# Local attention in 32-query tiles, division at the PV eviction, and norm per token, in a fused attention and two-MLP kernel

## The chip, the cores and the metric

One core of one Trainium2 chip runs the program. The metric is the device time of one execution in microseconds (us); lower is better.

## The reference

```python
# attention, B=4, H=8, Sl=512 local and Sg=32 global tokens, D=64, window 32
s_g = scale * q_g @ k_all.T                      # global queries see all 544 keys
out_g = sm(s_g) @ v_all
s_ll = where(|i - j| <= 32, scale * q_l @ k_l.T, -1e9)
a_l = sm(concat([scale * q_l @ k_g.T, s_ll]))    # local: 32 global keys and a band
out_l = a_l @ concat([v_g, v_l])
x = concat([out_g, out_l]) as (2176 tokens, 512)
# first MLP, F=1536
xn = x / sqrt(mean(x*x) + 1e-6) * rms_g
x = (silu(xn @ w_gate) * (xn @ w_val)) @ w_out
# second MLP, F=2048
out = (s * relu(x @ w_in)**2 + b) @ w_out
# sm(s) = exp(s - max) / (sum + 1e-9)
```

The weights come as 64-bit floats.

## The kernel before

**Dense part.** The 2176 tokens are cut into five groups of 512, 512, 512, 320 and 320 tokens (GROUPS). For each group 12 slots of the first MLP and 16 of the second run one after another; a slot is 128 hidden features. All dense products are split into a high and a low fp32r part and computed as three matmuls (`mm3`, L621 to L624): `emit_first` makes the hidden features into the PSUM tiles `m`, `emit_second` adds them into four banks `acc0` and `acc1`. There are 4128 dense matmuls. During group 0 the weights are loaded as 64-bit values (`load_raw`, into `wr`), converted on ScalarE and VectorE (`conv`, L162 to L198), kept in one of five tiles `wt`, and stored to a scratch `wsc` in DRAM, which the later groups read (`load_w`).

**Attention.** A unit is one batch and two heads. The units of batches 1, 2 and 3 (12 units with local tokens) and the four of batch 0 (global tokens alone) are worked off in small steps between the dense matmuls of the group before the one that needs them (`unit_steps`, `unit_queue`); odd units also do the 32 global queries of two units. The local tokens of batch 0 are done first, in `start`, in eight half units of 256 tokens. The steps of a unit are:

- `sc` (twice): 8 score matmuls of 64 queries by 160 keys (128 of the window, 32 global), both heads and two query blocks side by side in the array; four VectorE operations add the mask and take the minimum (L281).
- `st_e`: eight exponentials with row sums on ScalarE (L331). `st_r`, `st_n`, `glob`: reciprocals, division of the probabilities, on VectorE and ScalarE.
- `st_t` (twice): five transposes (L253, L254), one copy (L257). `st_v`: 16 matmuls of 64 by 64 for the window (L268) and 8 of 64 by 128 for the global keys (L276); the output is feature-major.
- odd units: `st_g`, `st_tg`, `st_gv` (L318, L359, L377) for the global queries.

`build_steps` makes the normed input `x` of a group: squares, one matmul with ones that sums over the partitions (L470; in group 0 four of 256 tokens for each half, L461), a reciprocal root over all tokens on all partitions, one scaling, and the high and low parts. In group 0 it runs once for each 256 tokens, so the first two slots start on the first half (`hs`).

**What sets the order.** The program text gives priorities (`hp`) and dependences; a scheduler that runs before the chip does fixes one order of instructions for each engine. SP issues all DMAs in one such order.

Of the kernel before, what the change touches and what calls it, by code (L numbers as in the profile page):

```python
# [24 lines left out]
KW = 160  # L25
VW = 9 * 128 + 64
# [17 lines left out]
C_ID = 3 * KW  # L44
# [13 lines left out]
SW = 256 + 4 * KW + 4 * 128 + 64  # L58
# [5 lines left out]
def attn_moe_kernel(ctx: ExitStack, tc: tile.TileContext, s0, q, k, v, w1, w2, cst, out):  # L64
# [43 lines left out]
    zeros = cp.tile([128, 128], F32, name="zeros")  # L108
    zw = zeros[:, 0:1].broadcast_to((128, 512))
    epsc = cp.tile([128, 1], F32, name="epsc")  # L110
    pm = cp.tile([128, 4, 2, KW], F32, name="pm")
    pg = cp.tile([128, 640], F32, name="pg")
    qf = cp.tile([128, 2, 64], F32, name="qf")
    ident = ct[:, C_ID:C_ID + 128]
    mask = [ct[:, C_MASK + i * KW:C_MASK + (i + 1) * KW] for i in range(3)]

    def cmask(c):
        return mask[0 if c == 0 else (2 if c == 3 else 1)]
# [88 lines left out]
    def u_tile(b):  # L207
        if b not in ut:
            ut[b] = u_p.tile([128, HP, 4, 128], F32, tag="u", name="u")
        return ut[b]  # L210
# [6 lines left out]
    def load_u(i):  # L217
        if i >= len(UNITS) or i in raw_u:
            return
        b, p, loc = UNITS[i]  # L220
        vr = at_p.tile([128, VW], F32, tag="vr", name="vr", bufs=2)
        e = ST if loc else SG
        qr = at_p.tile([128, ST], F32, tag="qr", name="fq")
        kr = kr_p.tile([128, 8, KW], F32, tag="kr", name="fk")
        nc.sync.dma_start(out=qr[:, 0:e], in_=q[b, p, :, 0:e])
        nc.sync.dma_start(out=kr, in_=k[b, p])
        nc.sync.dma_start(out=vr, in_=v[b, p])
        raw_u[i] = (qr, kr, vr)

    def scores(bk, qr, kr, q0, cs):  # L230
        mms = []
        for n, c in enumerate(cs):
            for e in range(2):
                for h in range(2):
                    x = slice(64 * h, 64 * h + 64)
                    i = 2 * c + e
                    mms.append(PE.matmul(bk[64 * e:64 * e + 64, h, n * KW:(n + 1) * KW],  # L237
                                         lhsT=qr[x, q0 + 64 * i:q0 + 64 * i + 64], rhs=kr[x, i]))
        in_turn(mms)

    def glob(p, rs):
        gl = pt_p.tile([128, 4, 32], F32, tag="gl", name="gl")
        V.tensor_tensor(out=gl, in0=p.rearrange("p c h n -> p (c h) n")[:, :, 128:KW],
                        in1=rs.rearrange("p (n o) -> p n o", o=1).broadcast_to((128, 4, 32)), op=ALU.mult)
        return gl.rearrange("p n k -> p (n k)")

    def transposes(bk, p, gl):
        flat = bk.rearrange("p b n -> p (b n)")
        mms = []
        for c in range(2):  # L250
            for h in range(2):
                o = 128 * (2 * c + h)
                mms.append(PE.transpose(flat[:, o:o + 128], p[:, c, h, 0:128], ident))  # L253
        mms.append(PE.transpose(flat[:, 512:640], gl, ident))  # L254
        in_turn(mms)
        t = pt_p.tile([128, 5, 128], F32, tag="pt", name="ptf")
        A.copy(out=t.rearrange("p a n -> p (a n)"), in_=flat[:, 0:640])  # L257
        return t

    def values(bk, vr, vg, pts):  # L260
        mms = []
        for c in range(2 * len(pts)):
            t = pts[c // 2]
            for e in range(2):
                for h in range(2):
                    i = 2 * c + e
                    o = 128 * (c // 2) + 64 * e
                    mms.append(PE.matmul(bk[64 * h:64 * h + 64, c % 2, o:o + 64],  # L268
                                         lhsT=vr[:, 128 * i + 64 * h:128 * i + 64 * h + 64],
                                         rhs=t[:, 2 * (c % 2) + h, 64 * e:64 * e + 64], start=(c < 2 and e == 0), stop=False))  # L270
        for c in range(2 * len(pts)):
            t = pts[c // 2]
            for h in range(2):
                x = slice(32 * (2 * (c % 2) + h), 32 * (2 * (c % 2) + h) + 32)
                o = 128 * (c // 2)
                mms.append(PE.matmul(bk[64 * h:64 * h + 64, c % 2, o:o + 128], lhsT=vg[x], rhs=t[x, 4],  # L276
                                     start=False, stop=(c // 2 == len(pts) - 1), tile_position=(x.start, 64 * h)))
        in_turn(mms)

    def neg_scaled(out_, in_, m, acc):  # L280
        V.tensor_tensor_reduce(out=out_, in0=in_, in1=m, scale=-0.125, scalar=3.0e38,  # L281
                               op0=ALU.add, op1=ALU.min, accum_out=acc)

    def norm_eng(out_, in_, sc_, e):
        if e == "A":
            A.mul(out=out_, in_=in_, mul=sc_)
        else:
            V.tensor_scalar(out=out_, in0=in_, scalar1=sc_, scalar2=None, op0=ALU.mult)

    def unit_steps(i):  # L290
# [4 lines left out]
        def prep():  # L295
# [5 lines left out]
            S["nm"] = sm_p.tile([128, 4, 2], F32, tag="nm", name="nm")  # L301
# [36 lines left out]
        def st_r():  # L338
# [3 lines left out]
            if not kp:  # L342
                return
# [458 lines left out]
```

## Time and profile before

| | us |
|---|---|
| median of 3 runs (range) | 996.46 (996.26 to 997.35) |
| span of the profiled execution | 995.6 |
| TensorE busy (PE) | 946.3 (95%) |
| weight loads busy (PEld) | 790.7 (79%) |
| VectorE busy (DVE) | 471.7 (47%) |
| ScalarE busy (ACT) | 464.9 (47%) |
| moved by DMA | 249.54 MB |

The page gives the span of the profiled execution, from its first to its last instruction, and no other time for it; the median of the runs lies 0.9 us above. The busy time of PE counts overlapping matmuls once. Matmul records of fp32 operands come in twos: one matmul instruction leaves two records. "at" is a two-bank PSUM tile that all attention steps share, "m" and "acc" hold dense results.

### The profile page before, as it was taken

Reading aid. Unit: us, or ns where it says so; the run is one execution under the profiler, and the core shown is the slowest. Engines: PE = TensorE matmul, PEld = TensorE weight load, DVE = VectorE, ACT = ScalarE, POOL = GpSimd, SP = SyncE. Lnnn points to the kernel's source line nnn. Section 1 sums busy time; section 2 is a strip of 40 time slices with the busy share of each in tenths; the row PEclk is TensorE's granted clock in tenths of the full one; section 3 lists DMA queues with packets and bytes.
Section 4 is the critical chain, followed back from the end, with each engine's and each line's share of the span. In section 5 each row is a group of like instructions: output and inputs, shape, how many; then the busy total and the mean of one; then the engine's idle time right before and its main releaser. Section 6 shows DMA issues by size and latency. Waiting matters only on the chain.

```text
span 995.6 us, 15191 instructions
## 1 busy us (share of the span) xinstructions
PE 946.3 (95%) x6024; PEld 790.7 (79%) x6024; DVE 471.7 (47%) x1149; ACT 464.9 (47%) x908; POOL 0.8 (0%) x9
## 2 busy tenths in 40 slices
PE   5758999889999999999999999999999999999998
PEld 4437777667877778777877878778789999999998
DVE  6995978769954141334353131443442243421322
ACT  5886697667744152533346252633441342311222
POOL 0000000000000000000000000000000000000000
PEclk9578999999999999999999999999999999999999
DMA  9985789848964754446565655346488848988584
GB/s 371 409 324 204 282 306 349 308 162 311 356 240 170 264 203 183 163 143 225 213 232 191 239 204 187 142 173 245 167 308 337 305 159 309 340 338 300 181 328 153
DMA packets 41110, 249.54 MB, mean 251 GB/s; under 512 B 5072, under 2 KB 6096, under 8 KB 23120
## 3 DMA queue, kind: packets, MB, share of 16 engines
q1 hardware_dynamic: 41040, 248.58, 67.4%
q8 instruction: 47, 0.77, 0.3%
q14 instruction: 23, 0.19, 0.0%
HBM read 208.46 MB, written 40.11 MB: 250 GB/s over the span
## 4 chain that ended last, share of the span: by engine, by line
PE 80%; DMA 7%; DVE 6%; ACT 5%; issue 1%; SPq 0%; ACTq 0%; DVEq 0%
PE m L622 15%; PE m L624 14%; PE m L623 14%; PE acc L622 10%; PE acc L623 10%; PE acc L624 10%; DMA wr<-in_w_dram 4%; DMA wt<-wsc 2%; PE at L237 2%; PE at L268 1%; ACT ce L177 1%; PE at L377 1%; PE at L253 1%; DVE wt L142 1%; DMA fq<-in_q_dram 1%
## 5 line engine op out<-in xcount | busy, mean ns | idle before, releaser
L623 PE MATMUL acc<-h,wt 128*128 128x512 f32 (+1 forms) x560 | 200.6, 359 | 1.4 <-DVE h L142 1.3
L624 PE MATMUL acc<-h,wt 128*128 128x512 f32 (+1 forms) x560 | 200.2, 358 | 0.0
L622 PE MATMUL acc<-h,wt 128*128 128x512 f32 (+1 forms) x560 | 192.5, 363 | 0.5 <-DVE y L142 0.3
L622 PE MATMUL m<-x,wt 128*128 128x512 f32 (+2 forms) x496 | 178.7, 362 | 11.3 <-ACT x L136 9.2
L623 PE MATMUL m<-x,wt 128*128 128x512 f32 (+2 forms) x496 | 175.8, 355 | 0.1
L624 PE MATMUL m<-x,wt 128*128 128x512 f32 (+2 forms) x496 | 175.3, 354 | 0.0
L622 PE MATMUL m<-y,wt 128*128 128x512 f32 (+1 forms) x320 | 117.0, 373 | 7.6 <-DVE t L711 4.2
L623 PE MATMUL m<-y,wt 128*128 128x512 f32 (+1 forms) x320 | 116.2, 364 | 2.9 <-DVE y L142 2.9
L623 PEld LDWEIGHTS acc<-h,wt 128*128 128x128 f32 x560 | 105.2, 188 | 15.3 <-DVE h L142 2.1
L622 PEld LDWEIGHTS acc<-h,wt 128*128 128x128 f32 x560 | 103.6, 188 | 16.3 <-issue 1.7
L624 PEld LDWEIGHTS acc<-h,wt 128*128 128x128 f32 x560 | 105.1, 188 | 13.6 <-issue 0.5
L624 PE MATMUL m<-y,wt 128*128 128x512 f32 (+1 forms) x320 | 115.4, 361 | 0.0
L622 PEld LDWEIGHTS m<-x,wt 128*128 128x128 f32 x496 | 93.9, 190 | 26.4 <-ACT x L136 9.9
L692 DVE TENSOR_TENSOR a<-sg,m 128x512 f32<-128x512 f32 (+1 forms) x60 | 36.4, 607 | 142.9 <-PE m L624 136.5
L624 PEld LDWEIGHTS m<-x,wt 128*128 128x128 f32 x496 | 93.9, 189 | 11.1 <-issue 0.3
L623 PEld LDWEIGHTS m<-x,wt 128*128 128x128 f32 x496 | 93.9, 189 | 10.8 <-DVE x L142 0.8
L711 DVE SCALAR_TENSOR_TENSOR t<-m,ct,r 128x512 f32<-128x512 f32 (+1 forms) x80 | 53.2, 670 | 98.3 <-ACT r L710 98.1
L710 ACT ACTIVATE r<-m 128x512 f32<-128x512 f32 (+1 forms) x80 | 42.1, 532 | 115.2 <-PE m L624 115.0
L685 ACT ACTIVATE sg<-m 128x512 f32<-128x512 f32 (+1 forms) x60 | 32.0, 534 | 96.9 <-PE m L624 96.7
L136 ACT CAST h<-a 128x512 fp32r<-128x512 f32 (+1 forms) x60 | 33.3, 555 | 92.2 <-DVE a L692 73.2
L622 PEld LDWEIGHTS m<-y,wt 128*128 128x128 f32 x320 | 59.8, 189 | 20.8 <-ACT y L136 4.4
L713 ACT ACTIVATE h<-t,ct 128x512 fp32r<-128x512 f32 (+1 forms) x80 | 52.2, 658 | 50.9 <-DVE t L711 33.1
(141 smaller groups left out, 1137.6 us busy)
## 6 DMA issues: line engine op xcount, KB each, us to landing
wt<-wsc SPq DMA_DIRECT2D x48, 1536.0 KB, 7.5
wt<-wsc SPq DMA_DIRECT2D x64, 1024.0 KB, 4.8
wr<-in_w_dram SPq DMA_DIRECT2D x68, 512.0 KB, 6.3
wsc<-wt SPq DMA_DIRECT2D x12, 1536.0 KB, 7.3
wsc<-wt SPq DMA_DIRECT2D x16, 1024.0 KB, 6.2
fk<-in_k_dram SPq DMA_DIRECT2D x16, 640.0 KB, 5.3
vr<-in_v_dram SPq DMA_DIRECT2D x16, 608.0 KB, 6.0
s_w<-in_s_dram SPq DMA_DIRECT2D x8, 736.0 KB, 11.5
```

Of the source, the lines that this page charges most:

```text
L136: A.copy(out=out_, in_=in_)
L142: V.tensor_tensor(out=dst_l, in0=src, in1=dst_h.bitcast(F32), op=ALU.subtract)
L177: A.copy(out=e.bitcast(I16), in_=odd)
L237: mms.append(PE.matmul(bk[64 * e:64 * e + 64, h, n * KW:(n + 1) * KW], lhsT=qr[x, q0 + 64 * i:q0 + 64 * i + 64], rhs=kr[x, i]))
L622: PE.matmul(out_, lhsT=wh, rhs=xh, start=first, stop=False)
L623: PE.matmul(out_, lhsT=wh, rhs=xl, start=False, stop=False)
L624: PE.matmul(out_, lhsT=wl, rhs=xh, start=False, stop=last)
L685: A.activation(out=sg[:, :N], in_=gb[:, :N], func=AF.Silu)
L692: V.tensor_tensor(out=a[:, :N], in0=sg[:, :N], in1=vb[:, :N], op=ALU.mult)
L710: A.activation(out=r[:, :N], in_=hb[:, :N], func=AF.Relu)
L711: V.scalar_tensor_tensor(out=t[:, :N], in0=hb[:, :N], scalar=ct[:, C_S:C_S + 1], in1=r[:, :N], op0=ALU.mult, op1=ALU.mult)
L713: A.activation(out=h[:, 0, :N], in_=t[:, :N], func=AF.Identity, bias=ct[:, C_B:C_B + 1])
```

## The change

A local unit is now one block. Queries go in 16 tiles of 32; each sees 64 keys before and 64 after a cut (96 of the window, 32 global: `key_window` takes them as two pieces of one key array, so the block has 128 columns and no separate global part). Scores are 32 matmuls of 32 rows by 128 columns into both banks. The mask is added to the 512 scores per row that need it, one reduction takes the maximum of the eight rows of 128, one subtraction writes all 1024 values, one exponential follows. Eight transposes and one copy turn the unnormed probabilities. PV is 32 matmuls of 32 rows by 65 columns, token-major; the 65th column of V is one and gives the row sum, and the division is done as the result is evicted. The input norm of a group is then a ScalarE square with a row sum per 128 tokens, a reciprocal root of a few columns, a scaling, and 16 transposes per 512 tokens (8 in the groups of 320) before the high and low parts are made. Global tokens get a small norm of their own (`gsq`). In `start` batch 0 is done in four whole units, with loads of its own from `q`, `k` and `v`; `build_steps(0)` runs once, over all 512 tokens. Global PV takes six key blocks in place of five.

```diff
-KW = 160
-VW = 9 * 128 + 64
+KN = 544
+KW = KN + 16 * 64
+VW = 130
+NW = 17
...
-    def scores(bk, qr, kr, q0, cs):
+    def scores(bk, qr, kr, q0):
         mms = []
...
+        for i in range(16):
+            c, g = divmod(i, 4)
+            for h in range(2):
+                x = slice(64 * h, 64 * h + 64)
+                mms.append(PE.matmul(
+                    bk[32 * g:32 * g + 32, h, 128 * c:128 * c + 128].rearrange("p (a n) -> p a n", a=2),
+                    lhsT=qr[x, q0 + 32 * i:q0 + 32 * i + 32], rhs=key_window(kr, x, i)))
         in_turn(mms)
...
+    def less_max(bk, pp):
+        sv = bk.rearrange("p h (c n) -> p (h c) n", n=128)
+        ends = sv.rearrange("p a (b n) -> p a b n", n=64)[:, :, :, 0:32]
+        mx = sm_p.tile([128, 8], F32, tag="mx", name="mx")
+        V.tensor_tensor(out=ends, in0=ends, in1=mask, op=ALU.add)
+        V.tensor_reduce(out=mx, in_=sv, axis=mybir.AxisListType.X, op=ALU.max)
+        V.tensor_tensor(out=pp, in0=sv, in1=mx.rearrange("p (a o) -> p a o", o=1).broadcast_to((128, 8, 128)),
+                        op=ALU.subtract)
...
+    def values(bk, vr, t, o):
         mms = []
...
+        for c in range(4):
             for h in range(2):
+                for g in range(4):
+                    mms.append(PE.matmul(bk[32 * g:32 * g + 32, h, 65 * c:65 * c + 65],
+                                         lhsT=t[:, 4 * h + c, 32 * g:32 * g + 32],
+                                         rhs=vr[:, 4 * c + g, 65 * h:65 * h + 65]))
         in_turn(mms)
...
+        V.tensor_scalar(out=rs, in0=po[:, :, :, 64], scalar1=1e-9, scalar2=None, op0=ALU.add)
+        V.reciprocal(out=rs, in_=rs)
+        V.tensor_tensor(out=o.rearrange("p c (h n) -> p h c n", h=2), in0=po[:, :, :, 0:64],
+                        in1=rs.rearrange("p h (c o) -> p h c o", o=1).broadcast_to((128, 2, 4, 64)), op=ALU.mult)
...
+        r = [(prep, 0.3)]
+        if not loc and not kp:
+            return r + [(lambda: load_u(i + 1), 0.0)]
+        if loc:
+            r += [(st_s, 0.8), (lambda: expo(pm), 2.5)]
+        if kp:
+            r += [(st_g, 0.8), (st_r, 1.5), (st_tg, 1.0), (st_gv, 1.5)]
+        if loc:
+            r += [(st_t, 1.5), (st_v, 1.5)]
+        return r
...
+        def turn(p0, p1):
+            bk = bank().rearrange("p a n -> p (a n)")
+            w = 128 * n
+            in_turn([PE.transpose(bk[:, w * (p - p0) + 128 * (c - c0):w * (p - p0) + 128 * (c - c0) + 128],
+                                  ut[b][:, c, 128 * p:128 * p + 128], ident) for p in range(p0, p1) for c in cs])
+            x = x_tile()
+            for p in range(p0, p1):
+                src = bk[:, w * (p - p0):w * (p - p0) + w]
+                gs = ct[:, C_G + p:C_G + p + 1]
+                A.mul(out=x[:, 0, p, 0:w], in_=src, mul=gs)
+                V.scalar_tensor_tensor(out=x[:, 1, p, 0:w], in0=src, scalar=gs, in1=x[:, 0, p, 0:w].bitcast(F32),
+                                       op0=ALU.mult, op1=ALU.subtract)
...
+            for p in range(HP):
+                PE.matmul(bk, lhsT=ones, rhs=s[:, p], start=(p == 0), stop=(p == HP - 1))
...
+        def ld(u, last=True):
+            qr, kr, vr = raw[u]
+            nc.sync.dma_start(out=qr, in_=q[0, u, :, SG:ST])
+            nc.sync.dma_start(out=kr, in_=k[0, u])
+            if u == 0:
+                nc.sync.dma_start(out=ct, in_=cst)
+            nc.sync.dma_start(out=vr[:, 0:16], in_=v[0, u, :, 0:16])
...
+        with hp(400):
+            for f in build_steps(0, nb):
+                f[0]()
         load_u(0)
```

Two places show how the orders of instructions move. The first is TensorE while group 1 is computed, at the end of an attention unit. Before, the second five transposes and the 24 PV matmuls (L622 to L624 are dense):

```order
L624 MATMUL m<-y,wt 128x512
L253 MATMUL at<-ct,pm 128x128 x4
L254 MATMUL at<-ct,gl 128x128
L622 MATMUL m<-y,wt 128x512 x2
L623 MATMUL m<-y,wt 128x512
L624 MATMUL m<-y,wt 128x512
L623 MATMUL m<-y,wt 128x512
L624 MATMUL m<-y,wt 128x512
L268 MATMUL at<-ptf,vr 64x64 x16
L276 MATMUL at<-ptf,vr 64x128 x8
L622 MATMUL m<-y,wt 128x512
```

Now (L548 to L550 are dense):

```order
L259 MATMUL at<-ct,pm 128x128 x8
L548 MATMUL m<-x,wt 128x512
...
L550 MATMUL m<-x,wt 128x512
L269 MATMUL at<-vr,ptf 32x65 x32
L548 MATMUL acc_2843<-h,wt 128x512
```

The eight transposes of a unit stand together, and its PV is one block of 32 narrow matmuls.

The second is ScalarE in the start, where the input `x` of group 0 is finished (L136 and L132 with `wt`, and L176, L177, L183 or L172, L173, L179, convert weights). Before, around the first casts of `x`:

```order
L136 CAST x<-xn 128x256 x2
L257 COPY ptf<-acc_552 128x640
L136 CAST wt<-cv 128x2x512
L176 ACTIVATE cv<-wr 128x1024
L177 COPY ce<-wr 128x2048
L136 COPY u<-at 128x256
L136 CAST x<-xn 128x256
```

Now, from the start of the conversion of slot 3 to the second write of `x`:

```order
L172 ACTIVATE cv<-wr 128x1024
L373 ACTIVATE r_535<-ss,epsc 128x4
L173 COPY ce<-wr 128x2048
L374 ACTIVATE r_535<-r_535 128x4
L179 ACTIVATE cv<-wr 128x512
L132 CAST wt<-cv 128x2x512
L172 ACTIVATE cv<-wr 128x1024
L173 COPY ce<-wr 128x2048
L414 ACTIVATE x<-at,ct 128x512
L132 CAST wt<-cv 128x512
L179 ACTIVATE cv<-wr 128x512
L414 ACTIVATE x<-acc_561,ct 128x512
```

The second L172 reads the raw weights of slot 4. It stands ahead of the first write of `x` (L414).

## Rows read from the trace of the kernel before

**Rows 1.** The page, part 2: TensorE busy, in tenths, in 40 slices of the span.

```profile
PE   5758999889999999999999999999999999999998
```

**Rows 2.** Windows: stretch, its length, busy by engine, TensorE clock, DMA share, GB/s.

```profile
0.00:25.00 25.00, 14.79 (x137) 10.17 (x137) 17.07 (x73) 14.27 (x45) 0.84 (x9) 0.99 0.94 372
25.00:50.00 25.00, 19.46 (x181) 12.44 (x181) 22.74 (x81) 21.28 (x51) 0.00 (x0) 0.50 1.02 408
50.00:75.00 25.00, 13.54 (x122) 9.90 (x122) 24.51 (x71) 20.74 (x44) 0.00 (x0) 0.70 0.85 323
...
500.00:800.00 300.00, 299.78 (x1832) 248.29 (x1831) 107.00 (x287) 119.95 (x248) 0.00 (x0) 1.00 0.61 226
...
900.00:925.00 25.00, 25.00 (x173) 25.00 (x172) 4.42 (x9) 4.29 (x10) 0.00 (x0) 1.00 0.79 280
```

**Rows 3.** Timeline of TensorE, a block of scores: start us, length, line, shape.

```profile
353.28 0.39 PE L624 MATMUL m<-x,wt 128*128 128x512 f32 x1
353.60 0.77 PE L237 MATMUL at<-fk,fq 64*64 64x160 f32 x16
...
354.64 0.40 PE L623 MATMUL m<-x,wt 128*128 128x512 f32 x1
```

**Rows 4.** The same, a block of five transposes.

```profile
390.06 0.39 PE L622 MATMUL m<-x,wt 128*128 128x512 f32 x1
390.30 0.60 PE L253 MATMUL at<-ct,pm 128*128 128x128 f32 x4
...
391.07 0.39 PE L624 MATMUL m<-x,wt 128*128 128x512 f32 x1
```

**Rows 5.** The same, a block of PV.

```profile
401.66 0.39 PE L623 MATMUL m<-x,wt 128*128 128x512 f32 x1
401.98 1.15 PE L268 MATMUL at<-ptf,vr 128*64 128x64 f32 x32
403.06 0.67 PE L276 MATMUL at<-ptf,vr 32*64 32x128 f32 x16
...
404.00 0.40 PE L622 MATMUL m<-x,wt 128*128 128x512 f32 x1
```

**Rows 6.** The same, the PV of the global queries, and dense matmuls without a block.

```profile
351.70 0.39 PE L623 MATMUL m<-x,wt 128*128 128x512 f32 x1
...
384.02 0.39 PE L623 MATMUL m<-x,wt 128*128 128x512 f32 x1
384.33 1.36 PE L377 MATMUL at<-pgt,vr 128*64 128x32 f32 x40
...
385.96 0.39 PE L622 MATMUL m<-x,wt 128*128 128x512 f32 x1
```

**Rows 7.** The page, part 6: the loads of the start, KB each.

```profile
wr<-in_w_dram SPq DMA_DIRECT2D x68, 512.0 KB, 6.3
...
s_w<-in_s_dram SPq DMA_DIRECT2D x8, 736.0 KB, 11.5
```

**Rows 8.** Timeline of ScalarE in the start: the conversions of slots 4 and 5.

```profile
54.80 1.13 ACT L176 ACTIVATE cv<-wr 128x1024 f32<-128x1024 f32 x1
...
65.38 1.89 ACT L177 COPY ce<-wr 128x2048 int16<-128x2048 int16 x1
```

**Rows 9.** Tile x in the start, and line L685, the silu of slots 0 to 2.

```profile
L142 DVE TENSOR_TENSOR x<-xn,x x8: 375/422/439, 54.1 to 81.5; 128x256 fp32r<-128x256 f32 x8
...
L685 ACT ACTIVATE sg<-m x3: 592/597/597, 84.2 to 97.1; 128x512 f32<-128x512 f32 x3
```

**Rows 10.** Lines by form: VectorE and ScalarE operations like those added and removed.

```profile
L711 DVE SCALAR_TENSOR_TENSOR t<-m,ct,r 128x512 f32<-128x512 f32 x48 | 35.7, 750 | 50.9 <-ACT r L710 50.6
L181 DVE SCALAR_TENSOR_TENSOR cv<-cv,ce 128x1024 int32<-128x1024 int32 x19 | 23.2, 1224 | 0.3
...
L178 DVE TENSOR_SCALAR cv<-cv 128x1024 f32<-128x1024 f32 x19 | 13.2, 693 | 8.5 <-ACT cv L176 8.5
...
L136 ACT CAST y<-acc 128x512 fp32r<-128x512 f32 x12 | 6.8, 582 | 0.8 <-PE acc L624 0.6
```

More of the change, by code (lines that the diff above doesn't have):

```diff
@@ L249, in transposes, with expo @@
+    def expo(pp):
+        A.activation(out=pp, in_=pp, func=AF.Exp, scale=0.125)
+    def transposes(bk, pp):
+        flat = bk.rearrange("p b n -> p (b n)")
+        in_turn([PE.transpose(flat[:, 128 * a:128 * a + 128], pp[:, a], ident) for a in range(8)])
+        t = pt_p.tile([128, 8, 128], F32, tag="pt", name="ptf")
+        A.copy(out=t.rearrange("p a n -> p (a n)"), in_=flat)
+        return t
+    def values(bk, vr, t, o):
         mms = []
-        for c in range(2):
+        for c in range(4):
@@ L255, in transposes @@
         in_turn(mms)
[L256 to L288, printed above, removed]
+        po = bk[:, :, 0:260].rearrange("p h (c n) -> p h c n", c=4)
+        rs = sm_p.tile([128, 2, 4], F32, tag="rs", name="rs")
@@ L300, in prep, with st_s @@
                 V.tensor_copy(out=qf[x, kp, SG * h:SG * (h + 1)], in_=qr[x, 0:SG])
[L301 to L307 removed]
+            S["gm"] = sm_p.tile([128, 4], F32, tag="gm", name="gm")
+        def st_s():
             bk = banks("at")
[L309 to L312 removed]
+            scores(bk, raw_u[i][0], raw_u[i][1], SG)
+            less_max(bk, pm)
         def st_g():
@@ L372, in st_gv @@
                 vr = raw_u[i - 1 + e][2]
-                for a in range(5):
+                for a in range(6):
+                    x = slice(0, 96 if a < 5 else 64)
                     for h in range(2):
                         o = bk[64 * h:64 * h + 64, SG * e:SG * e + SG]
-                        w = 128 * min(2 * a, 8) + 64 * h
-                        mms.append(PE.matmul(o, lhsT=vr[:, w:w + 64], rhs=t[:, a, e, h], start=(a == 0), stop=(a == 4)))
+                        mms.append(PE.matmul(o, lhsT=vr[x, 1 + 3 * a, 65 * h:65 * h + 64], rhs=t[x, a, e, h],
+                                             start=(a == 0), stop=(a == 5)))
             in_turn(mms)
@@ L510, in start @@
+        def ld(u, last=True):
[5 more added lines that the diff above has]
+            nc.sync.dma_start(out=vr[:, 0:16], in_=v[0, u, :, 0:16])
+        for u in range(HP):
+            place(u)
         ld(0)
-        nc.sync.dma_start(out=ct, in_=cst)
+        load_raw()
         ld(1)
@@ L532, in start @@
             PE.matmul(bk[:, 0:128], lhsT=ones, rhs=ones)
-        P = [pm[:, 0:2], pm[:, 2:4]]
-        P += [act_p.tile([128, 2, 2, KW], F32, tag="h", name="s_p") for _ in range(2)]
-        st = [cp.tile([128, 3, 4], F32, name=f"sst{i}") for i in range(8)]
+        P = [pm] + [act_p.tile([128, 8, 128], F32, tag="h", name="s_p") for _ in range(2)]
         bn = [0]
@@ L572, in V_ @@
[L572 to L595 removed]
+            scores(bk, raw[u][0], raw[u][1], 0)
@@ new lines, in S_, with T_, V_ @@
+            less_max(bk, P[u % 3])
+            expo(P[u % 3])
+        def T_(u):
+            pts[u] = transposes(nb(), P[u % 3])
+        def V_(u):
+            values(nb(), raw[u][2], pts[u], u_tile(0)[:, :, 128 * u:128 * u + 128])
+        cb = blocks[:6]
+        with hp(400):
+            S_(0)
+            S_(1)
+        for u in range(HP):
+            with hp(400):
+                T_(u)
+                if u + 2 < HP:
+                    S_(u + 2)
+                V_(u)
+            if u < 3:
+                conv(cb[u][0], cb[u][1], cb[u][1] + 1)
@@ L596, in start @@
+        with hp(400):
+            for f in build_steps(0, nb):
+                f[0]()
         load_u(0)
-        for f in bs[1][4:]:
-            f[0]()
         for i in range(3, 6):
```

407 lines of the change are left out of this document (136 added, 271 removed).

## The prediction

> **What bounds the kernel now.** I read three views in this order. First the page's slices [rows 1]: TensorE is busy at 9 tenths from the fifth slice on, and at 5, 7, 5 and 8 tenths in the first four, the first 100 us. So there are two stages with different limits. Second the windows [rows 2]. From 500 to 800 us TensorE is busy for 299.78 of 300 us while VectorE and ScalarE work 107 and 120 us: here only what TensorE itself executes costs time, and work moved off VectorE or ScalarE is worth nothing. In the first 75 us it is the reverse: TensorE is busy for 48 us, partly at the lower clock (granted 0.50, which is 1.2 GHz, from 25 to 50 us), VectorE for 17, 23 and 25 of each 25 us, and DMA stands at a share of 0.94, 1.02 and 0.85, with 372, 408 and 323 GB/s. Third the timeline of TensorE, for what an attention block costs in the saturated stage. A block's price is the distance between the dense matmuls around it less the distance that they have without it. That is 0.226 us: from the first of [rows 6] to the first of [rows 3] are 7 dense matmuls in 1.58 us.
>
> **TensorE, a local unit now.** Scores [rows 3]: two dense steps take 353.28 to 354.64 us, 1.36, less 0.45 is 0.91 us. The 8 matmuls leave 16 records of two array cycles per column: 320 cycles at 2.4 GHz are 0.133 us, 2.13 us one after another. As the block is 0.77 us long, four 64 by 64 tiles work side by side (0.53 us); the other 0.38 us is entering and leaving the small tiles. Five transposes [rows 4]: 1.01 less 0.45, 0.56 us, so 0.11 each and nothing for entering. PV [rows 5]: 2.34 less 0.45, 1.89 us. A unit pays 2 x 0.91 + 2 x 0.56 + 1.89 = 4.83 us.
>
> **A local unit after.** The trace has no tile of 32 columns; this is the one large unknown. Scores are 32 matmuls, 64 records of 128 columns, 0.107 us each. If the eight tiles of 64 by 32 work side by side, as four of 64 by 64 do now, that is 8 x 0.107 = 0.86 us, with the 0.38 us 1.24 us. PV is 64 records of 65 columns, 0.054 us, in four tiles: 0.87 + 0.38 = 1.25 us. Eight transposes: 0.89 us. Together 3.38 us. The lower bound is the array itself, without any cost of entering, 2.6 us. The upper bound comes from [rows 6]: the global PV has 40 records of only 32 columns, 0.027 us in two tiles, 0.53 us in all by columns, and takes 1.36 us, 0.034 us for each record. If that is a price per record whatever its width, 64 records cost 2.18 us, both blocks with 0.2 us at the edges 2.4 us each, and a unit 5.7 us. I take 3.38 us, because another row explains the 0.034 us by the width of the weights: from 900 to 925 us the weight loads are busy all 25 us, 172 of them, 0.145 us for 128 columns [rows 2]; 64 columns are then 0.073 us, and two tiles at once give 0.036 us per record. A weight of 32 columns in four or eight tiles would cost 0.009 us or less and stay hidden.
>
> So a unit saves 4.83 - 3.38 = 1.45 us, and the 12 local units 17.4 us. All lie in groups 0 to 2, where nothing on TensorE is hidden.
>
> **What TensorE pays in addition.** Global queries, eight times: PV has 24 matmuls in place of 20, the last of them on 64 rows, so 1.49 us [rows 6] becomes about 1.8; six transposes in place of five, 0.11 us. That is +0.4 x 8 = +3.2 us. The norm, four groups after the first: the matmul with ones costs 0.85 us of array time for 512 tokens (two records of 1024 cycles) and 0.53 us for 320. In its place stand 16 transposes, 1.76 us, in groups 1 and 2, and in groups 3 and 4 eight, 0.88 us, and 8 records of 64 columns with full weights at 0.145 us, 1.16 us. That is +0.9 x 2 + 1.5 x 2 = +4.8 us. The sum for TensorE is -17.4 + 3.2 + 4.8 = **-9.4 us**, between -19 and +18 with the bounds of a unit.
>
> **The start.** Before, x of the first 256 tokens is there early, the last of the second half at 81.5 + 0.4 us, and the silu of slot 2 stands at 97.1 us [rows 9]. From there on the dense part runs at its own pace, so I compare that point. After, x exists only when all four units are done. Every load of the start is larger: a unit brings 256 KB of q, 784 KB of k and 1040 KB of v, four of them 8320 KB, where eight times 736 KB were 5888 KB [rows 7]; unit 0 of batch 1, with the next unit's k and v, 4050 KB in place of 2768. The order on ScalarE puts the conversion of slot 4 ahead of the first write of x, so x waits for the fifteenth raw block of 512 KB. Ahead of its landing lie 8320 + 323 + 4050 + 15 x 512 + 2 x 1536 KB, 24.0 MB; before the change 20.2 MB. At the rates of [rows 2], 9.3 MB by 25 us and 19.5 MB by 50 us, the rest at about 370 GB/s, it lands at 62 us, where it was there at 54.8 us [rows 8]. Then follow on ScalarE the two conversions (1.13 and 1.89 us [rows 8]), four writes of x from PSUM at 0.58 us, three casts and conversions, and on VectorE the last of four operations of 0.75 us [rows 10]: x is complete at about 72 us. Six matmul parts of 2.7 us (12 x 0.226) lead to the silu of slot 2, 88 us, and some 3 us go to a TensorE that begins at the low clock: 91 in place of 97.1, **-6 us**. Bounds: if DMA ran at the 323 GB/s of the third window from the beginning, x would be complete at 84 us, +6 us. If raw weights were not late, VectorE would decide: ahead of the last write its order has 40 operations of 512 elements with two operands (0.75 us), 18 with one (0.35, half of 0.69), 14 and 8 of 1024 (1.22 and 0.69) [rows 10], 59 us, so x at 61 us, -17 us.
>
> **What I cost at nothing.** By the two orders VectorE falls from 1151 to 751 instructions and ScalarE from 774 to 574; their cover is the dense stream, and both had more than half of the 300 us free [rows 2]. A block now holds the shared PSUM tile for three VectorE operations, about 3.2 us in place of 1; if the next attention step came before, TensorE would stand still, but steps are paced up to 4 us apart. Later loads of a unit grow by 0.7 MB, 2.8 MB in group 0, under 10 us of the queue that runs beside the matmuls; if that cover went, raw weights would come late, which is a rival below.
>
> **The sum.** The profiled execution has a span of 995.6 us, and the median lies 0.9 us above it. 996.5 - 9.4 - 6 = **981 us**.
>
> **Rivals.** (1) Narrow tiles are bound by records, not by columns. Place: the 24 blocks of scores and PV; price 2.4 us each, a unit 5.7 in place of 4.83 us, 12 x 0.87 = +10.4, with the rest of TensorE +18; with the start 1009 us, slower. It decides from the point at which a block takes over 1.9 us. For it speaks the global PV [rows 6], which is far from its column time; against it that weight loads explain the same number. Chance 0.14. The Trainium skill speaks for this rival (TensorEngine Tiling (Array Packing), Performance Considerations): each matmul has about 60 cycles of overhead, and one should not take the tiling factor from a dimension that is already small. By its 60 cycles, 25 ns, a block would be an estimated 2.0 us, a unit 4.9 us, and the change about 999 us; the trace shows no block of this kind, and its scores block, 16 records in 0.53 us, does not contradict it.
> (2) Only half of the tiles work side by side (four for scores, two for PV): both blocks double their array time, 12 x 1.73 = +20.8, in all 1002 us. Against it: [rows 3] and [rows 5] show full use of two and four tiles. Chance 0.05.
> (3) The start comes later, at the upper bound, or raw weights run late in group 0: +12 us against the forecast, 993 us, at the edge of no change. For it: 24.0 in place of 20.2 MB and DMA shares near 1. Chance 0.14.
> (4) The start is bound by VectorE alone (-17 us), and blocks cost less at their edges than I take (-14 in place of -9.4 us on TensorE): 965 us. For it: VectorE is busy 23 and 25 of 25 us in the start [rows 2]; against it the loads. Chance 0.09.
>
> **Numbers.** The forecast, 0.58, has its own range from 970 to 991 us. A measurement of this kernel tells about 0.2%, 2 us, from no change. Faster: 0.58, rival 4, and 0.08 of rival 3, in all 0.75. Within 2 us: 0.06 of rival 3. Slower: rivals 1 and 2, 0.19. The range reaches up to part of rivals 1 and 2 and down to rival 4: 965 to 1003 us.
>
> **What would show it.** In the profile after: blocks of scores (L240 x64) and PV (L269 x64) near 1.1 us long and not 2.2; dense matmuls 0.226 us apart around them; the last write of x near 72 us and the silu of slot 2 near 91 us. The forecast is wrong if a block is over 1.9 us long, if x is complete after 80 us, or if TensorE waits for raw weights between 100 and 300 us for more than a few us above the present.

## The result, and the profile after

The changed kernel takes 979.43 us (median, 978.07 to 982.54) against 996.36 us for the kernel before on the same chip (995.09 to 997.35): a ratio of 0.9832, 95% interval 0.9814 to 0.9851. The profiled execution has a span of 976.8 us, 18.8 less than the one of before; the medians differ by 16.9, and the forecast was 15.4. What follows takes the two profiled executions apart, so its parts add up to 18.8. The total came out near the forecast (981). Its parts did not: two terms came out too small, and a third, which the forecast did not have, made up for both.

The first view is the page, part 2, of the changed kernel: TensorE busy in tenths, in 40 slices (compare [rows 1]).

```profile
PE   4439999899999999999999999999999999999998
```

The windows of the changed kernel, with the columns of [rows 2]:

```profile
0.00:25.00 25.00, 11.41 (x237) 8.96 (x238) 12.11 (x17) 7.46 (x9) 0.58 (x7) 0.93 0.95 378
25.00:50.00 25.00, 11.25 (x317) 9.24 (x315) 22.45 (x42) 13.79 (x17) 0.00 (x0) 0.70 1.01 414
50.00:75.00 25.00, 9.34 (x58) 7.42 (x58) 20.80 (x38) 19.15 (x28) 0.00 (x0) 0.57 0.89 361
500.00:800.00 300.00, 298.88 (x2133) 251.91 (x2132) 94.26 (x179) 97.06 (x156) 0.00 (x0) 1.00 0.61 222
```

There are still two stages: the start, in which TensorE now works for only 32 of 75 us, and the saturated rest. What an attention block costs is in TensorE's timeline, which answers to [rows 3 to 6]: eight transposes, PV (x64), scores (x64), and the global PV (x48), each with the last dense matmul before it and the second behind it.

```profile
359.05 0.39 PE L548 MATMUL m<-x,wt 128*128 128x512 f32 x1
359.29 1.04 PE L259 MATMUL at<-ct,pm 128*128 128x128 f32 x8
...
360.39 0.40 PE L550 MATMUL m<-x,wt 128*128 128x512 f32 x1
...
365.39 0.39 PE L548 MATMUL acc<-h,wt 128*128 128x512 f32 x1
365.70 1.12 PE L269 MATMUL at<-vr,ptf 128*32 128x65 f32 x64
...
367.10 0.39 PE L550 MATMUL acc<-h,wt 128*128 128x512 f32 x1
...
375.28 0.39 PE L550 MATMUL acc<-h,wt 128*128 128x512 f32 x1
375.60 1.16 PE L240 MATMUL at<-fk,fq 64*32 64x128 f32 x64
...
377.02 0.40 PE L549 MATMUL acc<-h,wt 128*128 128x512 f32 x1
...
352.39 0.39 PE L549 MATMUL m<-x,wt 128*128 128x512 f32 x1
352.71 1.95 PE L338 MATMUL at<-pgt,vr 96*64 96x32 f32 x48
...
354.93 0.40 PE L548 MATMUL m<-x,wt 128*128 128x512 f32 x1
```

Less the 0.45 us of two dense steps these are 0.89, 1.26, 1.29 and 2.09 us. A local unit costs 3.44 us on TensorE (forecast 3.38, before 4.83): 12 x -1.39 = -16.7 us. The global queries cost 0.70 us more per pair of units (PV +0.60, transposes 0.66 in place of 0.56), eight times +5.6 (forecast +3.2). The norm's transposes and the matmuls with ones add 4.4 (forecast 4.8). TensorE's sum is -6.7 us (forecast -9.4).

The start, tile x of the changed kernel (VectorE's last operations on it) and its first silus, against [rows 9]:

```profile
L415 DVE SCALAR_TENSOR_TENSOR x<-acc,ct,x x2: 743/744/744, 69.3 to 72.1; 128x512 fp32r<-128x512 f32 x2
...
L611 ACT ACTIVATE sg<-m x3: 595/597/597, 77.5 to 96.8; 128x512 f32<-128x512 f32 x3
```

x is complete at 72.8 us (forecast 72), but the silu of slot 2 stands at 96.8 us, where 91 was forecast and 97.1 was before. Measured at a point that both dense streams share, the 111th dense matmul, the lead is 3.3 us (93.9 to 90.6), not 6.

That leaves 8.8 us of the 18.8, and no term of the forecast had them. If one adds up the gaps of over 0.62 us from the start of one record of TensorE to the start of the next, behind the 111th dense matmul and each less 0.3 us, before has 16.2 us of idle time and the change 7.3. Of the 8.9 us between them 6.5 lie in group 0, up to the 865th dense matmul, and 2.3 behind it. The line between this term and TensorE's own is not sharp: such a gap can hold a part of a block, which the sum of prices above counts too. The waits of TensorE from 98 to 320 us show the larger part (for what, us in total, times, longest), first before:

```profile
PE m L622 <- DVE t L711: 2.9, 2, 2.3
PE m L623 <- DVE y L142: 2.9, 2, 2.1
PE m L622 <- ACT y L136: 1.9, 2, 1.0
PE acc L623 <- DVE h L142: 1.3, 2, 1.0
```

and in the changed kernel:

```profile
PE m L548 <- ACT y L132: 2.8, 1, 2.8
PE at L303 <- DVE pm L251: 1.5, 1, 1.5
PE m L548 <- DVE t L637: 0.3, 1, 0.3
```

So start -3.3, TensorE -6.7, idle -8.9: -18.9 us, against -18.8 measured.

### The profile page after: what moved, and what is told of

The parts are those of the page before. It is cut to its first block, busy times and chain, and to the rows that moved or that the text cites. A ratio compares the mean times of both kernels' runs of the same rounds, so it can differ in the third digit from the quotient of the medians.

```text
span 976.8 us, 16209 instructions
## 1 busy us (share of the span) xinstructions
PE 921.7 (94%) x6888; PEld 785.1 (80%) x6888; DVE 444.0 (45%) x749; ACT 409.7 (42%) x596; POOL 0.6 (0%) x7
## 4 chain that ended last, share of the span: by engine, by line
PE 83%; DMA 7%; DVE 6%; ACT 3%; issue 1%; SPq 1%; ACTq 0%; DVEq 0%
PE m L548 15%; PE m L550 15%; PE m L549 15%; PE acc L548 11%; PE acc L549 10%; PE acc L550 10%; DMA wr<-in_w_dram 6%; PE at L338 2%; PE at L269 2%; PE at L240 1%; DVE wt L138 1%; PE at L259 1%; DVE cv L183 1%; ACT ce L173 1%; PE at L303 1%
## 5 line engine op out<-in xcount | busy, mean ns | idle before, releaser
L550 PE MATMUL acc<-h,wt 128*128 128x512 f32 (+1 forms) x560 | 200.2, 358 | 0.0
L548 PE MATMUL acc<-h,wt 128*128 128x512 f32 (+1 forms) x560 | 194.3, 366 | 0.2 <-ACT z L132 0.2
L548 PE MATMUL m<-x,wt 128*128 128x512 f32 (+2 forms) x496 | 177.2, 358 | 1.6 <-DVE a L618 1.4
L550 PE MATMUL m<-x,wt 128*128 128x512 f32 (+2 forms) x496 | 175.3, 354 | 0.0
L548 PE MATMUL m<-y,wt 128*128 128x512 f32 (+1 forms) x320 | 113.8, 363 | 5.4 <-ACT y L132 3.2
L548 PEld LDWEIGHTS acc<-h,wt 128*128 128x128 f32 x560 | 103.6, 188 | 15.9 <-issue 1.6
L550 PEld LDWEIGHTS acc<-h,wt 128*128 128x128 f32 x560 | 105.3, 188 | 13.2
L549 PE MATMUL m<-y,wt 128*128 128x512 f32 (+1 forms) x320 | 115.1, 360 | 0.0
L550 PE MATMUL m<-y,wt 128*128 128x512 f32 (+1 forms) x320 | 114.8, 359 | 0.0
L548 PEld LDWEIGHTS m<-x,wt 128*128 128x128 f32 x496 | 93.6, 189 | 15.1 <-DVE a L618 1.6
L550 PEld LDWEIGHTS m<-x,wt 128*128 128x128 f32 x496 | 94.0, 189 | 10.8
L132 ACT CAST h<-a 128x512 fp32r<-128x512 f32 (+1 forms) x60 | 33.3, 556 | 119.2 <-DVE a L618 107.3
L640 DVE SCALAR_TENSOR_TENSOR h<-t,ct,h 128x512 fp32r<-128x512 f32 (+1 forms) x80 | 53.1, 670 | 57.1 <-ACT h L639 56.8
```

The costliest lines, as they stand in the source:

```text
L132: A.copy(out=out_, in_=in_)
L548: PE.matmul(out_, lhsT=wh, rhs=xh, start=first, stop=False)
L549: PE.matmul(out_, lhsT=wh, rhs=xl, start=False, stop=False)
L550: PE.matmul(out_, lhsT=wl, rhs=xh, start=False, stop=last)
L640: V.scalar_tensor_tensor(out=h[:, 1, :N], in0=t[:, :N], scalar=ct[:, C_B:C_B + 1], in1=h[:, 0, :N].bitcast(F32), op0=ALU.add, op1=ALU.subt ...
```

## The experiments

Twelve kernels were run. Each is compared by its ratio to the kernel before on its own chip, where the change has 0.9832; 0.001 is 1 us. Three questions: are narrow tiles priced by columns, what did the idle time go by, and what bounds the start?

**Tiles side by side.** The first two runs only change the order of matmuls within a block.

```diff
-        for i in range(16):
-            c, g = divmod(i, 4)
-            for h in range(2):
+        for h in range(2):
+            for i in range(16):
+                c, g = divmod(i, 4)
```

> The change with the score matmuls of a unit in another order: all sixteen blocks of 32 queries of the first head, then all of the second, so that consecutive matmuls have four places to go to and not eight. Theory of columns: in the trace of the changed kernel eight records start together every 109 ns (64 records in 0.89 us); with four at a time the same 64 records need 16 steps of 109 ns = 1.74 us, so the block goes from 1.29 to about 2.15 us, and the time rises by 12 x 0.86 = 10 us, with the four units of the start up to 13: 989 to 993 us against 979.4. Rival, price per record whatever the tiles: the block stays at 1.3 us and the time at 979 to 981.

Measured: 983.33 us, ratio 0.9878 (0.9856 to 0.9900), so +4.6 us to the change. TensorE's timeline of this kernel:

```profile
379.55 0.39 PE L550 MATMUL acc<-h,wt 128*128 128x512 f32 x1
379.87 1.56 PE L240 MATMUL at<-fk,fq 64*32 64x128 f32 x64
...
381.70 0.39 PE L549 MATMUL acc<-h,wt 128*128 128x512 f32 x1
```

The block costs 1.70 us in place of 1.29, 12 x 0.41 = 4.9 us. The order counts, so a price per record alone is out; but the step is half of what I expected. The single records tell why: at both ends of the block four start per 109 ns; in the middle, from 0.46 to 0.84 us, fours start every 26 to 83 ns, so the second head's matmuls have begun before the first's are through, and more than four run at once.

```diff
-        for c in range(4):
-            for h in range(2):
-                for g in range(4):
+        for g in range(4):
+            for c in range(4):
+                for h in range(2):
```

> The change with the PV matmuls of a unit in another order: the sixteen matmuls of one column tile one after another, so that consecutive matmuls go to the same 32 columns. Theory of columns: the trace of the changed kernel has four records every 55 to 58 ns (64 in 0.91 us); on one tile each would take about 55 ns by itself, 64 of them 3.5 us, so the block goes from 1.26 to about 3.9 us and the time rises by 12 x 2.6 = 31 us, with the start up to 42: 1010 to 1021 us. Rival, price per record (or weight loads as the bound): the block stays at 1.3 us, the time at 979 to 982.

Measured: 994.42 us, ratio 0.9990 (0.9977 to 1.0002), so +15.7 us.

```profile
365.69 0.39 PE L548 MATMUL acc<-h,wt 128*128 128x512 f32 x1
366.01 3.25 PE L269 MATMUL at<-vr,ptf 128*32 128x65 f32 x64
...
369.53 0.40 PE L550 MATMUL acc<-h,wt 128*128 128x512 f32 x1
```

PV costs 3.39 us in place of 1.26: four tiles side by side save 2.1 us per unit, and rival 1 of the prediction falls with rival 2. Yet 12 x 2.13 = 25.6 us went in and only 15.7 came out. This kernel's 111th dense matmul starts at 80.3 us, 10.3 earlier than in the change, although its start has more to compute. The order that the scheduler chose for this kernel is another one: VectorE begins the fourth pair's softmax at 31.5 us in place of 35.9, ahead of conversions that stood before it. That is followed up below.

**The global PV.** Its single records come in pairs every 58 ns, as before the change. But at three places in the block the rows change from 96 to 64 or back (the expectation counts four), and there the next pair starts 156 to 160 ns after the last, and the one after it after 79.

```diff
-    pg = cp.tile([128, KN], F32, name="pg")
+    pg = cp.tile([128, 576], F32, name="pg")
...
-                    x = slice(0, 96 if a < 5 else 64)
+                    x = slice(0, 96)
```

> The change with the last block of keys of the global rows padded from 64 to 96 rows (32 zero columns behind the probabilities; the values have zero rows there already), so that all 24 PV matmuls of a pair of units have 96 rows, with one copy of 96 x 768 in place of two, and six transposes of 96 rows. Theory of the switch: in the trace of the changed kernel the pairs of records follow each other by 58 ns, except where the rows change from 96 to 64 or back (153 and 79 ns, four such places in a block); without them the block is 24 x 0.058 + 0.3 = about 1.7 us in place of 2.09, the transposes stay at 0.66, and the time falls by 8 x 0.37 = 3 us, to 976 to 977. Rival, price per record: 48 records stay 48, the block stays at 2.1 us, the time at 979 to 980.

Measured: 977.43 us, ratio 0.9816 (0.9798 to 0.9834).

```profile
351.63 0.39 PE L548 MATMUL m<-x,wt 128*128 128x512 f32 x1
351.95 1.59 PE L336 MATMUL at<-pgt,vr 96*64 96x32 f32 x48
...
353.81 0.39 PE L547 MATMUL m<-x,wt 128*128 128x512 f32 x1
```

The same 48 records, now without a change of rows, cost 1.73 us in place of 2.09, so the extra is the change of shape. Over the run TensorE's blocks shrink by 3.3 us; the time fell by 1.6 by the ratios, which is inside their intervals. The Trainium skill (TensorEngine Tiling (Array Packing), Key Properties) says that a change of the tiling mode, not merely of the tile, drains TensorE. The trace agrees, with 0.12 us each time: going from 96 to 64 rows, or back, costs what such a change would; that TensorE drains there, the records do not show.

**The idle time in group 0.** First a miss; `load_q` issues the load of the next queries alone.

```diff
+            if c0:
+                load_q(i + 1)
```

> The kernel before with one thing moved: the next unit's queries are loaded as soon as the scores of this unit have read theirs, not behind its PV. In the trace of before VectorE stands from 194.3 to 202.5 us on the copy of these queries, whose load was issued at 194.3, and the dense stage waits 7.2 us for VectorE's Y behind it. Theory of the late load: that stall goes, the idle time of TensorE behind the third silu falls from 15.3 to about 8 us and the time from 996.4 to 989 to 992; then the like part of what the change gained is a matter of where a load lands, not of less work for VectorE. Rival, VectorE has too much to do in this stage: the copy's wait goes and the dense stage waits for VectorE as long: 995 to 997.

Measured: 995.62 us, ratio 0.9996 (0.9985 to 1.0007): nothing. The expectation rests on a misreading. VectorE does not stand from 194.3 to 202.5 us; its rows there are conversions, the softmax of a unit and the low part of Y, one behind the other, and only at the end it waits, 1.06 us for an Exp and then 0.81 us for this load, as the row of before says. Nor could the load move: its buffer is free only when the scores have read the old queries, and it was issued at 192.9 in place of 194.3 us. The waits of TensorE are those of before.

```profile
202.45 0.37 DVE L300 COPY qf<-fq 64x32 f32<-64x32 f32 x2 [0.81 <-DMA fq<-in_q_dram]
```

What remains is that the two engines have much to do, which the next run tests by putting work back.

```diff
+        for a in range(8):
+            A.activation(out=pp[:, a], in_=pp[:, a], func=AF.Exp, scale=0.125, accum_out=es[:, a:a + 1])
+        for a in range(4):
+            V.tensor_scalar(out=pp[:, 2 * a], in0=pp[:, 2 * a], scalar1=1.0, scalar2=None, op0=ALU.mult)
+            A.mul(out=pp[:, 2 * a + 1], in_=pp[:, 2 * a + 1], mul=1.0)
```

> The change with work on ScalarE and VectorE put back into the softmax of the twelve units behind the start, of the size that before had: eight Exp of 128 columns with sums in place of one of 1024 (in the trace of before eight take 3.3 us, the one of the change takes 1.06), and four products with 1.0 on each of the two engines (1.28 us on ScalarE in before). TensorE's work is the same. Theory of relief: the dense stage waited less after the start because ScalarE and VectorE had less to do; TensorE's idle time from the 110th dense matmul on, 16.2 us before and 7.3 us in the change, comes back to 12 to 16 us and the time rises by 5 to 9 us, to 984 to 988. Rival, the idle time went because the work fell at other places of the order: it stays at 6 to 9 us, the time at 978 to 981.

Measured: 989.52 us, ratio 0.9921 (0.9899 to 0.9944), +8.9 us. TensorE's attention blocks cost the same (0.88, 1.25 and 1.29 us); its idle time behind the 111th dense matmul is 14.2 us in place of 7.3. The other 2.0 us come before it (92.6 us in place of 90.6), where the first unit's longer Exps already stand. The longest waits from 98 to 320 us are for the same two engines as before:

```profile
PE m L556 <- ACT y L132: 3.5, 2, 2.4
PE m L557 <- DVE y L138: 1.9, 1, 1.9
```

So 6.8 of the 8.9 us of idle time come back with the work. What was relieved is above all ScalarE: from 98 us to the 817th dense matmul it was busy for 139.8 us before, for 130.6 in the change and for 138.5 here; VectorE for 154.4, 152.6 and 154.8. Two things keep this from being a full proof. In group 0 only 3.3 of the 6.5 us come back, the other 3.5 lie behind it. And work put back also moves the order: the first two runs of the start below have the same work as each other, and TensorE's gaps between the 111th and the 817th dense matmul sum to 5.4 and 15.2 us. Relief is the likelier cause and this run bears it out; how much of the 8.9 us is order stays open.

**The start.** In the change VectorE has this order in the start (a few rows of its timeline; L249 to L251 are the softmax of the fourth pair of heads, L138, L183 and L185 conversions of weights; those of the second slot are wanted from 80 us on):

```profile
32.61 0.69 DVE L183 SCALAR_TENSOR_TENSOR cv<-wr,cv 128x512 int32<-128x512 int32 x1
...
35.88 0.69 DVE L249 TENSOR_TENSOR at<-at,ct 128x512 f32<-128x512 f32 x1
36.48 0.68 DVE L138 TENSOR_TENSOR wt<-cv,wt 128x512 fp32r<-128x512 f32 x1
37.08 0.68 DVE L185 SCALAR_TENSOR_TENSOR cv<-wr,cv 128x512 int32<-128x512 int32 x1
...
40.43 1.21 DVE L251 TENSOR_TENSOR pm<-at,mx 128x1024 f32<-128x1024 f32 x1
```

The scores lie ready at 31 us. Three runs hold conversions behind the softmax (a dependency in order alone, on the same engine); all three have the padded global rows.

```diff
-                conv(cb[u][0], cb[u][1], cb[u][1] + 1)
+                conv(cb[u][0], cb[u][1], cb[u][1] + 1, gate=gates[3] if u == 2 else None)
...
+                if i == 0:
+                    in_turn([marks["xl"], cq])
```

> The change, with the padded global rows of the third run (977.4 us), and with two things of the start put behind: the conversion of the third block of weights is placed on ScalarE behind the Exp of the fourth pair of heads, and the copy of the next unit's queries on VectorE behind the last write of x. In the trace of the change VectorE does 9.9 us of conversions and that copy while the scores of the fourth pair lie ready (31 to 41 us), and x is complete at 72.8 us. Theory of order: the start is bound by the chain from the fourth pair's scores to x, and what stands between them on VectorE delays the first dense matmul; x complete at 62 to 65 us, the first dense matmul at 57 to 60 (66.0), the time lower by 6 to 10 us, 967 to 971. Rival, the start is bound by the weights (their loads and conversions): x comes early, the silu of the third slot stays at 95 to 97 us and the time at 975 to 978.

> As the run before it, and the conversions of the second slot's weights are placed behind as well: its first block behind the fourth pair's Exp, its other two and with them the later slots behind the last write of x on ScalarE. Theory of order: x is complete at 54 to 58 us, the first dense matmul starts at 49 to 53 and the time is 4 to 8 us lower still, 960 to 967. Rival, the weights then bind: two or three conversions of 2.9 us on VectorE stand between x and the second slot, the silu of slots 1 to 3 come no earlier than in the run before, and the time is the same or up to 5 us longer.

> Between the two runs of the start: the third block and the whole second slot are converted behind the fourth pair's Exp (not behind x), and the third slot behind the last write of x. In the run with all conversions last the dense stage was 22 us ahead at its 110th matmul, but the queues moved only 140 GB/s between 50 and 75 us (raw weights wait for their buffers), and 15 us were lost again before group 1 began (275.5 us, against 272.3 in the run with one block held back). Theory of the weights' supply: with the buffers freed early the transfers go on (over 300 GB/s between 50 and 75 us), the first dense matmul starts at 53 to 57 us, little is given back, group 1 begins at 264 to 269 us, and the time is 958 to 964 us. Rival, group 0 is filled by VectorE's conversions whatever their order: group 1 begins at 271 to 275 us and the time is 966 to 970.

The conversions' `gate` is an instruction of ScalarE that must stand ahead of them: `gates[3]` the fourth pair's Exp, `marks["x"]` the last write of x. The second's edit is `gate=gates[3] if i == 3 else marks["x"]` at the second slot's conversions, the third's `gate=gates[3]` there and `marks["x"]` for the third slot. Starts in us; ratios with their intervals. The expectations call the 817th dense matmul the beginning of group 1. It is not: the first two slots of group 0 run in halves, so that group has 864, and the 817th still belongs to it. As a point that all kernels share it serves as well.

| kernel | last write of x | 111th dense | 817th dense | time, us | ratio |
|---|---|---|---|---|---|
| before | 81.5 | 93.9 | 294.1 | 996.36 | 1 |
| the change | 72.1 | 90.6 | 282.5 | 979.43 | 0.9832 (0.9814 to 0.9851) |
| one block held back | 67.7 | 84.6 | 272.3 | 967.17 | 0.9706 (0.9676 to 0.9735) |
| second slot behind x | 52.7 | 68.6 | 275.5 | 968.97 | 0.9718 (0.9695 to 0.9741) |
| in between | 57.7 | 74.2 | 275.0 | 968.19 | 0.9735 (0.9708 to 0.9762) |

All three are faster than both kernels, by 8 to 11 us against the padded change, and none can be told from another; the first, 967.17 us, is the fastest version found that leaves nothing out. Its time came as forecast, though x was complete only at 68.4 us (forecast 62 to 65). In the other two the start came as forecast or earlier, and the time did not: they end where the rivals had them. x came up to 19 us earlier with the very same loads, so the loads do not bound x. But of a lead of 22 us at the 111th dense matmul 7 are left at the 817th. The windows from 50 to 75 us, first of the run with one block held back, then of the one with the second slot behind x, and last of the one in between:

```profile
50.00:75.00 25.00, 14.70 (x131) 12.08 (x132) 24.08 (x42) 21.49 (x32) 0.00 (x0) 0.67 0.98 383
```

```profile
50.00:75.00 25.00, 24.63 (x209) 21.39 (x209) 23.60 (x40) 22.30 (x27) 0.00 (x0) 0.97 0.40 140
```

```profile
50.00:75.00 25.00, 22.50 (x194) 19.89 (x195) 19.78 (x37) 16.91 (x21) 0.00 (x0) 0.87 0.60 234
```

TensorE is filled earlier, the queues emptied. What SP, which issues all loads in one order, waits for from 45 to 75 us (us in total, times, longest) differs, first in the run with the second slot behind x, then in the one in between:

```profile
SPq L153 <- DVE cv L186: 29.9, 2, 18.4
```

```profile
SPq L223 <- DVE qf L291: 11.7, 1, 11.7
```

In the first, raw weights (L153) wait for buffers that late conversions do not free. In the second it is the other edit that holds the queue: the load of the next queries (L223) waits for the copy that is held behind x, then 5.2 us for scores, and is issued at 64.0 us; between 46.2 and 67.5 us no raw weights are issued. So the theory of the weights' supply was not tested: its condition, over 300 GB/s, did not come about, and the run without the copy held was not made. Which of the two edits of the first run made the start shorter, one run alone says:

> The change itself (without the padding) with only the copy of the next unit's queries held behind the last write of x, the conversions where the change has them. Theory that the conversions delayed the start: VectorE has no gap before that copy in the trace of the change (34.2 to 34.5 us), so the start stays as it is, 978 to 981 us. Rival, the copy was what held VectorE: 970 to 973.

Measured: 977.63 us, ratio 0.9820 (0.9797 to 0.9842), and x, the 111th and the 817th dense matmul all within 0.2 us of the change. So it was the conversions, alone or together with the copy. And the kernel before, with a like order?

> The kernel before with the same order in its start: the conversion of the third block of weights, and with it the second slot's, behind the last Exp of the start's eight half pairs. Theory that the start of before is bound by the same order: x is complete 5 to 10 us earlier and the time falls to 987 to 992 us, so that the start's gain of the last runs belongs to the order and not to the change. Rival, the start of before is bound by its own softmax work on VectorE and ScalarE, which the change lessens: x comes at most 2 us earlier, or the weights come late, and the time is 994 to 1000.

Measured: 997.22 us, ratio 1.0012 (1.0001 to 1.0024). Its 111th dense matmul did come 5.0 us earlier, as the first theory said; but the 817th starts at 297.6 us, 3.5 later than before, and the 865th, by count the first of group 1, at 310.0 against 309.7. Between the 111th and the 817th TensorE's gaps sum to 17.0 us in place of 11.4. So the first theory had the start right and the time wrong: there the lead is lost again in group 0. The order was worth 10 us in the kernel of the change and nothing in the kernel before; that the relief makes the difference fits this, but the two edits are not the same and no run shows it.

What, then, fills group 0? The last two runs start from the one in between.

```diff
-                V.tensor_scalar(out=g, in0=g, scalar1=W_LO, scalar2=W_HI, op0=ALU.max, op1=ALU.min)
```

> The run in between, and the clamp of each conversion of the weights (VectorE, 0.69 us of 1024 columns and 0.43 of 512) is left out, so the kernel does not bound the weights' exponents; per slot of the first kind 1.1 us less on VectorE, some 25 us less over group 0, with loads and stores as they are. In that run VectorE is busy 223 of the 274.6 us until group 1 begins, the queues 0.89 of them, and the start's lead of 16 to 22 us is mostly lost between the 600th and the 816th dense matmul. Theory that the conversions of VectorE fill group 0: it begins group 1 at 260 to 268 us, and the time is 955 to 962. Rival, the transfers fill it: group 1 begins at 272 to 276 us, the time 966 to 970.

```diff
-            nc.sync.dma_start(out=wsc[n], in_=w[:, 0:nb_].bitcast(F32))
+            nc.sync.dma_start(out=wsc[n], in_=w[:, 0:nb_, 0].bitcast(F32))
```

> The run in between, and of the converted weights only the high part is stored and loaded again twice, as high and as low part (the later groups then compute with wrong low parts); per slot 0.77 MB less for the queues, some 17 of 94 MB until group 1 begins; the work of all engines is the same. Theory that the transfers fill group 0: the raw weights come earlier, group 1 begins at 260 to 268 us, the time is 955 to 962. Rival, VectorE's conversions fill it: group 1 begins at 272 to 276 us, the time 966 to 970.

Measured: with less conversion 962.84 us, ratio 0.9661 (0.9644 to 0.9677), the 817th dense matmul at 269.1 us in place of 275.0: up to there VectorE was busy 21 us less, and 5.9 came out, less than I expected. With half the store 980.27 us, 0.9831 (0.9808 to 0.9853): the queues moved 74.9 MB in the first 275 us in place of 94, and it was 10 to 12 us slower (by the ratios, by the medians). Fewer bytes did not help, so transfers alone do not fill group 0; that the kernel became slower looks like an accident of order. VectorE's timeline of that kernel, then TensorE's:

```profile
195.86 1.21 DVE L138 TENSOR_TENSOR wt<-cv,wt 128x1024 fp32r<-128x1024 f32 x1
196.99 1.21 DVE L252 TENSOR_REDUCE mx<-at 128x8 f32<-128x1024 f32 x1
198.12 1.21 DVE L178 SCALAR_TENSOR_TENSOR cv<-cv,ce 128x1024 int32<-128x1024 int32 x1
199.26 1.40 DVE L640 SCALAR_TENSOR_TENSOR t<-m,ct,r 128x512 f32<-128x512 f32 x2
```

```profile
200.05 0.79 PE L551 MATMUL m<-y,wt 128*128 128x512 f32 x1 [2.86 <-DVE t L640]
200.65 0.63 PE L552 MATMUL m<-y,wt 128*128 128x512 f32 x1
201.07 0.63 PE L553 MATMUL m<-y,wt 128*128 128x512 f32 x1
```

t, for which the dense stage waits, stands behind two conversions and a maximum. How much of group 0 is VectorE's work and how much its order stays open: less work gave 5.9 of 21 us, and every edit also reordered. Both runs also keep the held copy, which stops the queue in the start.

## Why the prediction was right, and where it was not

**The unit.** Right: -16.7 of a forecast -17.4 us. Columns and tiles side by side price the blocks. The single records say it most plainly: eight of the scores start every 109 ns (forecast 107), in the first half of the block together, four of PV every 56 to 61 (54). The Trainium skill's 60 cycles per matmul (TensorEngine Tiling (Array Packing), Instruction Overhead) are an estimated 25 ns each. The prediction counted them for every record, 1.6 us for 64; the trace has 64 records of the scores from first start to last in 0.89 us, so this is out. Counted for every matmul of two records they are an estimated 0.8 us for 32, which 0.89 us alone does not contradict. What decides is that the same 32 matmuls of PV cost 1.26 or 3.39 us by their order: the price goes by columns and tiles.

**The global PV.** The term was mis-sized, 1.8 forecast and 2.09 measured. The step that failed took the 24 matmuls for alike; the last of each sum has 64 rows where the others have 96, and the run with 96 rows everywhere gives 1.73. The transposes, 0.11 forecast and 0.10 measured, were right.

**The start.** "The order on ScalarE puts the conversion of slot 4 ahead of the first write of x, so x waits for the fifteenth raw block": the numbers fell as worked out (block landed and conversion begun at 62.0, x complete at 72.8), and they led to only 3.3 of the 6 us at the point where it counts. As an explanation the step is wrong, and that the numbers agree is luck. That conversion reads the thirteenth and fourteenth block, there at 59.5 and 60.8 us, and began without a wait; and behind it ScalarE still waited for the transposes of x, which came last:

```profile
65.29 0.69 ACT L414 ACTIVATE x<-at,ct 128x512 fp32r<-128x512 f32 x1 [0.32 <-PE at L408]
```

With the same bytes x is complete as early as 53 us when conversions stand behind the softmax. It was VectorE's order, nearer to rival 4, which had 61 us for VectorE alone.

**What I cost at nothing.** This step failed, by 8.9 us. The cover that I named, both engines more than half free, was read in the window from 500 to 800 us, while the work that left was that of groups 0 to 2. In group 0 VectorE and ScalarE convert weights beside it, and before the change they were busy for 154.4 and 139.8 of the 196 us from 98 us to the 817th dense matmul. There the waits of TensorE are for them, and 6.8 us of idle time came back in the run with the work put back. The -9.4, -6 and 0 of the forecast became -6.7, -3.3 and -8.9: that the sum came out near is luck, as the third made up for the other two.

## What to carry to other kernels

Read the cover of a term in the very stage where its work lies, not in the cleanest window. Price narrow matmuls by columns and by how many tiles the order keeps going at once, and keep the shape of tiles the same through a block. Where a scheduler sets an engine's order, look in the trace for late work that stands ahead of urgent work; holding it back was worth 10 us here, and nothing in the kernel before. And look at what a held operation holds in turn: one late copy stopped the loads of all that stood behind it in SP's order.

## What was not expected

An idle TensorE pays twice. In the run with half the store TensorE works for 1.53 of the 5 us from 195 to 200; from 200 to 205 us the granted clock is 0.50, which is the 1.2 GHz level, and dense matmuls follow each other by 0.43 us in place of 0.226. The window view of that kernel, two stretches:

```profile
195.00:200.00 5.00, 1.53 (x6) 0.67 (x4) 5.00 (x7) 2.66 (x4) 0.00 (x0) 0.91 0.90 262
200.00:205.00 5.00, 4.95 (x12) 3.88 (x13) 3.05 (x4) 1.46 (x3) 0.00 (x0) 0.50 0.76 265
```

So some microseconds of waiting in group 0 cost more than their length. A second surprise is that with a slower PV the start was 10 us shorter; what the trace shows for it is the other order that the scheduler then chose.
